# Moving layernorm preparation into the QKV loop, mask setup to GpSimd, and PSUM buffers between pools

## Chip, cores, metric

The kernel runs on one core of one Trainium2 chip. The metric is the device time of one execution in microseconds (us); lower is better. The profiler records one execution, whose span is 1.7 to 2 us shorter than its device time. Runs that the record marks as slow (over 1.5% above the fastest of the same kernel) are left out. The granted clock is the share of the full TensorE clock that the trace records. In the text TensorE is the matmul engine, VectorE, ScalarE and GpSimd the elementwise ones; profile lines call them PE, DVE, ACT and POOL, and PEld is the load of matmul weights.

## The reference

```
x: 2048 x 640;  h = x + A(layernorm(x));  out = h + B(layernorm(h))

A(x): qkv = x @ wqkv                       # 640 x 1920, 32 heads of 20
      phi(t) = where(t > 0, t + 1, exp(t)) + 1e-6
      kv = sum_s phi(k) v^T ;  z = sum_s phi(k)       # per head
      o  = (phi(q) @ kv) / (phi(q) . z + 1e-6) ;  return o @ wo
B(x): token MLP along the 2048 axis: layernorm, w1 (2048 x 1728), gelu, w2
```

## The kernel before

The kernel is written for a framework that orders the instructions of every engine itself at build time: the order of the source is a priority, an instruction with lower priority may be put earlier if it looks ready, and each engine then runs its list strictly in that order. PSUM is the memory that the matmuls here write to; this program uses eight banks of it. PSUM tiles come from pools; a pool with `bufs=1` lets a new tile begin only when the last reader of the old one is done.

Only the first third, up to the "strips" (`pk^T @ [v | 1]` per head block), matters here. x is handled in four chunks of 512 rows. Each chunk is transposed raw, 20 groups of four transposes in all, each group copied out of PSUM by ScalarE. The layernorm is applied to the transposed data: mean and reciprocal deviation are broadcast over the partitions by a matmul with ones, copied out, then subtracted and multiplied in by VectorE.

```
with psT bufs=2, psM bufs=1 (tiles psMb, psRb):            # banks 0-3
    for n in range(4):                                      # chunk
        for c in range(5):
            psT = ...; 4 x nc.tensor.transpose(psT, x_nat ...)
            nc.scalar.activation(out=xnT[n][:, c], in_=psT, Copy)
        RHSM = mean * ident ; RHSR = rstd * ident           # VectorE
        matmul(psMb, ones, RHSM); Mb[n] = copy(psMb)        # ScalarE copy
        matmul(psRb, ones, RHSR); Rb[n] = copy(psRb)
        xnT[n] -= Mb[n] ; xnT[n] *= Rb[n]                   # VectorE
psQ bufs=4 (banks 0-3), psK bufs=1 (4-5), psV bufs=1 (6-7)
def phi_evac(psum, dst):
    tp = max(psum, 0) + 1e-6          # VectorE
    e  = exp(psum)                    # ScalarE
    dst = min(e, 1) + tp              # VectorE
for n in range(4):
    for tt in range(4):               # tile of 128 rows
        psK = 5 + 5 matmuls; phi_evac(psK, pk[t])
        psV = 5 + 5 matmuls; Vpp[t] = copy(psV)             # ScalarE
        js = [tt] if tt < 3 else [tt, 4]                    # five Q groups per chunk
        for j in js: psQ = 5 matmuls; phi_evac(psQ, pqT[n][:, j])
    if n == 1: build_masks()          # memsets on VectorE, selects on GpSimd
# ... cut ...
psStrip (5 one-bank tiles, banks 0-4): for k in 16: for i in 5: matmul(strip[i], pk[k], Vpp[k])
KVd, ZBd = strips * Mask              # VectorE
```

## Time and profile before

| reading | value | view |
|---|---|---|
| time | 295.12 us, median of 6 | runs |
| span of the profiled run | 293.1 us | page |
| TensorE / VectorE / ScalarE busy | 86% / 58% / 35% | page, part 1 |
| first K matmul | 25.67 us | timeline |
| first K result read by VectorE | 34.37 us | timeline |
| first Q matmul | 34.78 us | timeline |
| strips begin | 98.81 us | timeline |

The two groups of the MLP, which the change does not touch, are the largest. They come from part 5 of the page: line, engine, operation, output from inputs, shape, count, then busy us and mean ns, then idle us before it and what ended that idle time.

```profile
L381 PE MATMUL pu<-hn,w_sb 128*128 128x512 bf16 (+1 forms) x448 | 62.9, 304 | 5.3 <-DVE hn L352 5.3
L405 PE MATMUL py<-uT,w_sb 128*128 128x512 bf16 x448 | 64.2, 299 | 0.9 <-ACT xb L384 0.9
```

The front is best read from the timeline: start, duration, engine, source line, operation, count of merged instructions, and in brackets the idle time before it with what ended it. First ScalarE and VectorE up to the first K matmul, then what TensorE does.

```profile
13.40 1.05 ACT L163 ACTIVATE xnT_122<-psT 128x512 bf16<-128x512 bf16 x2
14.65 1.08 ACT L163 ACTIVATE xnT_122<-psT 128x512 bf16<-128x512 bf16 x2 [0.19 <-PE psT L162]
...
19.88 0.30 ACT L140 ACTIVATE rstd_78<-MV_77,eps_t 128x12 f32<-128x12 f32 x1 [4.14 <-DVE msq L135]
21.80 1.49 DVE L174 TENSOR_TENSOR xnT_122<-xnT_122,Mb_126 128x2560 bf16<-128x2560 bf16 x1
23.80 1.49 DVE L176 TENSOR_TENSOR xnT_122<-xnT_122,Rb_130 128x2560 bf16<-128x2560 bf16 x1
25.67 0.81 PE L227 MATMUL psK<-wqkv,xnT_122 128*128 128x512 bf16 x3
...
33.28 0.59 PE L235 MATMUL psV<-wqkv,xnT_122 128*128 128x512 bf16 x2 [1.56 <-ACT Vpp L240]
34.37 0.82 DVE L188 TENSOR_SCALAR tp<-psK 128x640 bf16<-128x640 f32 x1
```

The first chunk's subtraction (L174) runs at 21.80 and its multiplication (L176) at 23.80, and K starts at 25.67. The K result, complete at about 27.8, is read at 34.37, because VectorE works through the later chunks' preparation in between. The end of the QKV part:

```profile
95.02 2.32 PE L246 MATMUL psQ<-xnT_125,wqkv 128*128 128x512 bf16 x10
...
98.81 0.23 PE L271 MATMUL strip_1108<-Vpp,pk 128*128 128x168 bf16 x1 [1.47 <-ACT e L191]
```

The last two Q groups run back to back (10 matmuls in 2.32 us), and the strips then wait 1.47 us, until the last Q has been read.

### The profile page before, as it was taken

To read this page: it belongs to the slowest core of one execution; us is meant where nothing else is said; L and a number is where in the kernel's file an instruction comes from. 1 tells how busy PE (TensorE), PEld (TensorE's weight loads), DVE (VectorE), ACT (ScalarE), POOL (GpSimd) and SP (SyncE) were. 2 spreads that over 40 slices of the span, in tenths; PEclk is the share of its full clock that TensorE was granted. 3 is DMA by queue.
4 is the path that set the end of the run, shared out by engine and by line. 5 is a ranking of instruction groups with operands and counts; after the bars stand their busy time and mean duration, and the time that the engine had idled before them with its cause. 6 is when DMAs were issued, how large, how long until landed. Compare 5 with 4: busy or idle time off the path is not lost.

```text
span 293.1 us, 4250 instructions
## 1 busy us (share of the span) xinstructions
PE 253.1 (86%) x1736; PEld 136.8 (47%) x1736; DVE 171.3 (58%) x326; ACT 102.3 (35%) x166; POOL 26.2 (9%) x42
## 2 busy tenths in 40 slices
PE   0149799999999766998882999999998999999994
PEld 0125454555555642444441555555555555555552
DVE  3799997997787436887887554454544321222221
ACT  2949845545554202751224543334333000000000
POOL 8100070000000100003335000000000000000000
PEclk9999999999999997999997799999999999999998
DMA  6990000000000299100001994000000011110111
GB/s 216 362 229 1 2 1 19 0 0 2 0 0 2 58 425 421 65 0 2 0 0 17 392 410 154 0 0 2 0 2 0 22 47 45 47 45 35 35 45 45
DMA packets 13058, 23.07 MB, mean 79 GB/s; under 512 B 4304, under 2 KB 9136, under 8 KB 13040
## 3 DMA queue, kind: packets, MB, share of 16 engines
q1 hardware_dynamic: 4960, 12.41, 11.8%
q0 software_dynamic: 5216, 6.96, 8.6%
q10 hardware_dynamic: 2864, 3.44, 3.3%
q8 instruction: 13, 0.21, 0.3%
q14 instruction: 5, 0.04, 0.0%
HBM read 20.06 MB, written 2.62 MB: 77 GB/s over the span
## 4 chain that ended last, share of the span: by engine, by line
PE 73%; DVE 12%; ACT 7%; DMA 4%; POOL 2%; issue 2%; ACTq 0%; DVEq 0%
PE py L405 22%; PE pu L381 21%; PE psQ L246 5%; PE psV L235 4%; PE psK L227 4%; PE psN L317 4%; PE pa L329 4%; DMA x_nat<-in_A_x_dram 4%; DVE tp L188 2%; ACT e L191 2%; POOL h_nat L337 2%; PE psR L311 2%; DVE RDENQ L301 1%; PE psK L230 1%; PE psV L238 1%
## 5 line engine op out<-in xcount | busy, mean ns | idle before, releaser
L381 PE MATMUL pu<-hn,w_sb 128*128 128x512 bf16 (+1 forms) x448 | 62.9, 304 | 5.3 <-DVE hn L352 5.3
L405 PE MATMUL py<-uT,w_sb 128*128 128x512 bf16 x448 | 64.2, 299 | 0.9 <-ACT xb L384 0.9
L381 PEld LDWEIGHTS <-w_sb 128*128 128x128 bf16 (+1 forms) x448 | 35.3, 100 | 32.8 <-issue 7.7
L405 PEld LDWEIGHTS <-w_sb 128*128 128x128 bf16 x448 | 33.1, 97 | 32.0 <-issue 9.3
L408 DVE SCALAR_TENSOR_TENSOR ot<-py,b2col,h_nat 128x640 bf16<-128x640 f32 x16 | 14.1, 884 | 48.1 <-PE py L405 48.1
L162 PE MATMUL psT<-ident,x_nat 128*128 128x128 bf16 x80 | 9.4, 263 | 13.6 <-DMA x_nat<-in_A_x_dram 6.8
L384 ACT ACTIVATE xb<-pu,b1col 128x640 bf16<-128x640 f32 (+1 forms) x14 | 11.1, 794 | 20.9 <-PE pu L381 20.9
L162 PEld LDWEIGHTS <-x_nat 128*128 128x128 bf16 x80 | 7.3, 120 | 21.3 <-issue 13.6
L191 ACT ACTIVATE e<-psK 128x640 bf16<-128x640 f32 x16 | 11.3, 703 | 14.4 <-DVE tp L188 14.3
L191 ACT ACTIVATE e<-psQ 128x512 bf16<-128x512 f32 x20 | 12.0, 598 | 11.8 <-DVE tp L188 11.8
L192 DVE SCALAR_TENSOR_TENSOR pk<-e,tp 128x640 bf16<-128x640 bf16 x16 | 13.1, 817 | 5.1 <-ACT e L191 4.9
L337 POOL TENSOR_TENSOR h_nat<-hpre,x_nat 128x640 bf16<-128x640 bf16 x8 | 11.2, 1394 | 45.9 <-ACT hpre L336 45.9
L313 ACT ACTIVATE rexp<-psR 128x512 bf16<-128x512 f32 x20 | 11.7, 596 | 9.9 <-PE psR L311 9.8
L188 DVE TENSOR_SCALAR tp<-psK 128x640 bf16<-128x640 f32 x16 | 13.1, 820 | 2.5 <-PE psK L230 1.9
L188 DVE TENSOR_SCALAR tp<-psQ 128x512 bf16<-128x512 f32 x20 | 13.6, 686 | 0.5 <-PE psQ L246 0.4
L240 ACT ACTIVATE Vpp<-psV 128x640 bf16<-128x640 f32 x16 | 11.2, 703 | 4.9 <-PE psV L238 4.9
L246 PEld LDWEIGHTS <-wqkv 128*128 128x128 bf16 x100 | 9.1, 98 | 8.0
L336 ACT ACTIVATE hpre<-pa 128x640 bf16<-128x640 f32 x8 | 5.6, 703 | 20.3 <-PE pa L329 20.3
L393 DVE TENSOR_SCALAR th<-th 128x640 bf16<-128x640 bf16 (+1 forms) x14 | 4.6, 327 | 11.2 <-ACT th L392 11.2
L317 PEld LDWEIGHTS <-KVd 128*128 128x128 bf16 x52 | 5.3, 103 | 8.8 <-issue 4.0
L395 DVE TENSOR_TENSOR uT<-th,xb 128x640 bf16<-128x640 bf16 (+1 forms) x14 | 6.9, 492 | 0.5
L271 PEld LDWEIGHTS <-pk 128*128 128x128 bf16 x80 | 5.9, 97 | 1.9 <-issue 1.8
(277 smaller groups left out, 373.1 us busy)
## 6 DMA issues: line engine op xcount, KB each, us to landing
w_sb<-in_B_w_dram SPq DMA_DIRECT2D x1, 3584.0 KB, 18.7
w_sb<-in_B_w_dram SPq DMA_DIRECT2D x1, 3456.0 KB, 20.9
w_sb<-in_B_w_dram POOLq DMA_DIRECT2D x1, 3456.0 KB, 19.1
w_sb<-in_B_w_dram POOLq DMA_DIRECT2D x1, 3072.0 KB, 20.6
wqkv<-in_A_wqkv_dram SPq DMA_DIRECT2D x1, 2400.0 KB, 17.8
x_nat<-in_A_x_dram ACTq DMA_DIRECT2D x2, 640.0 KB, 8.8
x_nat<-in_A_x_dram SPq DMA_DIRECT2D x2, 640.0 KB, 7.8
out_dram<-ot SPq DMA_DIRECT2D x8, 160.0 KB, 1.8
```

The lines of the kernel that those rows point to most:

```text
L162: nc.tensor.transpose(psT[:, tt * P:(tt + 1) * P], x_nat[:, t, c * P:(c + 1) * P], ident[:])
L188: nc.vector.tensor_scalar(out=tp[:, 0:cols], in0=psum_ap, scalar1=0.0, scalar2=1e-6, op0=ALU.max, op1=ALU.add)
L191: nc.scalar.activation(out=e[:, 0:cols], in_=psum_ap, func=ACT.Exp)
L192: nc.vector.scalar_tensor_tensor(out=dst_ap, in0=e[:, 0:cols], scalar=1.0, in1=tp[:, 0:cols], op0=ALU.min, op1=ALU.add)
L227: nc.tensor.matmul(psK[:, 0:CH], lhsT=xn[:, c, tsl], rhs=wqkv[:, c, D:D + CH], start=(c == 0), stop=(c == NC - 1))
L235: nc.tensor.matmul(psV[:, 0:CH], lhsT=xn[:, c, tsl], rhs=wqkv[:, c, 2 * D:2 * D + CH], start=(c == 0), stop=(c == NC - 1))
L246: nc.tensor.matmul(psQ[:, :], lhsT=wqkv[:, c, j * P:(j + 1) * P], rhs=xn[:, c, :], start=(c == 0), stop=(c == NC - 1))
L317: nc.tensor.matmul(psN[:, :], lhsT=KVd[:, i, P * j:P * (j + 1)], rhs=pqT[n][:, i, :], start=(a == 0), stop=(a == len(ii) - 1))
L337: nc.gpsimd.tensor_tensor(out=h_nat[:, t, :], in0=hpre[:], in1=x_nat[:, t, :], op=ALU.add)
L381: nc.tensor.matmul(pu[:Mm, c0:c1], lhsT=w1_sb[:, k, m * P:m * P + Mm], rhs=hn[:, k, c0:c1], start=(k == 0), stop=(k == NT - 1))
L405: nc.tensor.matmul(py[:, c0:c1], lhsT=w2_sb[:Kk, k, t * P:(t + 1) * P], rhs=uT[:Kk, k, c0:c1], start=(k == 0), stop=(k == NF - 1))
L408: nc.vector.scalar_tensor_tensor(out=ot[:], in0=py[:, 0:D], scalar=b2col[:, t:t + 1], in1=h_nat[:, t, :], op0=ALU.add, op1=ALU.add)
```

## The change

The intent: let QKV start while later chunks are still being prepared, and take mask setup off VectorE. Chunks 0 and 1 are prepared ahead of the loop, chunks 2 and 3 inside it. The PSUM pools must now live at the same time, and all eight banks are taken: transposes go from two buffers to one, Q accumulators from four to one.

```
+    nc.gpsimd.memset(KVd[:], 0.0)      # ... ZBd, Mask, EselP, selects, DMAs: all on GpSimd, at the start
...
+    psT_pool = ...(name="psT", bufs=1)      # was 2
+    psM_pool = ...(name="psM", bufs=1)      # psMb, psRb: two banks, as before
+    psQ_pool = ...(name="psQ", bufs=1)      # was 4
+    psK_pool, psV_pool = ... bufs=1         # as before
+    for n in range(NCH):                    # all transposes and their copies, before the square roots
+        for c in range(NC): ...
     nc.scalar.activation(out=rstd1a ...Sqrt) ; reciprocal ; rstd1 likewise
+    for m in (0, 1): prep_rhs(m); prep_mm(m); prep_sub(m); prep_mul(m)
     for n in range(NCH):
+        m = n + 2
         for tt in range(TPC):
             ... K, V, Q as before ...
-        if n == 1: build_masks()
+            if m < NCH:
+                if tt == 0:   prep_rhs(m)
+                elif tt == 1: prep_mm(m); prep_sub(m)
+                elif tt == 2: prep_mul(m)
```

More of the change, by code (lines that the diff above doesn't have):

```diff
@@ L83 @@
     EselP = [pC.tile([P, NC, P], BF, name=f"EselP{q}") for q in range(NQ)]
+    nc.gpsimd.memset(KVd[:], 0.0)
+    nc.gpsimd.memset(ZBd[:], 0.0)
+    nc.gpsimd.memset(Mask[:], 1.0)
+    for i in range(NC):
+        mv = Mask[:, i, :].rearrange("p (h e) -> p h e", e=Dh + 1)
+        nc.gpsimd.affine_select(out=mv, in_=mv, pattern=[[-Dh, HPB], [0, Dh + 1]],
+                                compare_op=ALU.is_ge, fill=0.0, base=P * i - Dh * h0[i],
+                                channel_multiplier=1)
+        nc.gpsimd.affine_select(out=mv, in_=mv, pattern=[[Dh, HPB], [0, Dh + 1]],
+                                compare_op=ALU.is_ge, fill=0.0, base=Dh * h0[i] + Dh - 1 - P * i,
+                                channel_multiplier=-1)
+    for q in range(NQ):
+        nc.gpsimd.memset(EselP[q][:], 0.0)
+    nc.gpsimd.memset(EselP[0][0:H], 1.0)
+    for j in range(NC):
+        ev = EselP[0][0:H, j, :]
+        nc.gpsimd.affine_select(out=ev, in_=ev, pattern=[[1, P]], compare_op=ALU.is_ge, fill=0.0,
+                                base=P * j, channel_multiplier=-Dh)
+        nc.gpsimd.affine_select(out=ev, in_=ev, pattern=[[-1, P]], compare_op=ALU.is_ge, fill=0.0,
+                                base=Dh - 1 - P * j, channel_multiplier=Dh)
+    for q in range(1, NQ):
+        nc.gpsimd.dma_start(out=EselP[q][q * H:(q + 1) * H, :, :], in_=EselP[0][0:H, :, :])
     esR1 = ctx.enter_context(ExitStack())
@@ L137 @@
                                    in1=msq[:], op0=ALU.mult, op1=ALU.subtract)
-    nc.scalar.activation(out=rstd1a[:, :], in_=MVa[:, 1, :], func=ACT.Sqrt, bias=eps_t[:], scale=1.0)
-    nc.vector.reciprocal(out=rstd1a[:, :], in_=rstd1a[:, :])
-    nc.scalar.activation(out=rstd1[:, 0:NDV], in_=MV1[:, 0:NDV, 1:2], func=ACT.Sqrt, bias=eps_t[:], scale=1.0)
-    nc.vector.reciprocal(out=rstd1[:, 0:NDV], in_=rstd1[:, 0:NDV])
     def mean_ap(n):
@@ L151, in rstd_ap @@
         return rstd1a[:, :, None]
-    with tc.tile_pool(name="psT", bufs=2, space=bass.MemoryType.PSUM) as psT_pool, \
-            tc.tile_pool(name="psM", bufs=1, space=bass.MemoryType.PSUM) as psM_pool:
-        for n in range(NCH):
-            xn = xnT[n]
-            tsl_n = slice(n * TPC, (n + 1) * TPC)
-            for c in range(NC):
-                psT = psT_pool.tile([P, CH], BF, name="psT")
-                for tt in range(TPC):
-                    t = n * TPC + tt
-                    nc.tensor.transpose(psT[:, tt * P:(tt + 1) * P], x_nat[:, t, c * P:(c + 1) * P], ident[:])
-                nc.scalar.activation(out=xn[:, c, :], in_=psT[:, :], func=ACT.Copy)
-            nc.vector.tensor_tensor(out=RHSM[:, tsl_n, :], in0=mean_ap(n).to_broadcast([P, TPC, P]),
-                                    in1=ident[:, None, :].to_broadcast([P, TPC, P]), op=ALU.mult)
-            nc.vector.tensor_tensor(out=RHSR[:, tsl_n, :], in0=rstd_ap(n).to_broadcast([P, TPC, P]),
-                                    in1=ident[:, None, :].to_broadcast([P, TPC, P]), op=ALU.mult)
-            psMb = psM_pool.tile([P, CH], F32, name="psMb")
-            nc.tensor.matmul(psMb[:, :], lhsT=ones_bf[:, :], rhs=RHSM[:, tsl_n, :], start=True, stop=True)
-            nc.scalar.activation(out=Mb[n][:, :], in_=psMb[:, :], func=ACT.Copy)
-            psRb = psM_pool.tile([P, CH], F32, name="psRb")
-            nc.tensor.matmul(psRb[:, :], lhsT=ones_bf[:, :], rhs=RHSR[:, tsl_n, :], start=True, stop=True)
-            nc.scalar.activation(out=Rb[n][:, :], in_=psRb[:, :], func=ACT.Copy)
-            nc.vector.tensor_tensor(out=xn[:], in0=xn[:], in1=Mb[n][:, None, :].to_broadcast([P, NC, CH]),
-                                    op=ALU.subtract)
-            nc.vector.tensor_tensor(out=xn[:], in0=xn[:], in1=Rb[n][:, None, :].to_broadcast([P, NC, CH]),
-                                    op=ALU.mult)
-            if "xnT" in dbg:
-                nc.sync.dma_start(out=dbg["xnT"].rearrange("(c p) s -> p c s", p=P)[:, :, n * CH:(n + 1) * CH],
-                                  in_=xn[:])
@@ L182 @@
-    psQ_pool = esR4.enter_context(tc.tile_pool(name="psQ", bufs=4, space=bass.MemoryType.PSUM))
+    psT_pool = esR4.enter_context(tc.tile_pool(name="psT", bufs=1, space=bass.MemoryType.PSUM))
+    psM_pool = esR4.enter_context(tc.tile_pool(name="psM", bufs=1, space=bass.MemoryType.PSUM))
+    psQ_pool = esR4.enter_context(tc.tile_pool(name="psQ", bufs=1, space=bass.MemoryType.PSUM))
     psK_pool = esR4.enter_context(tc.tile_pool(name="psK", bufs=1, space=bass.MemoryType.PSUM))
     psV_pool = esR4.enter_context(tc.tile_pool(name="psV", bufs=1, space=bass.MemoryType.PSUM))
+    for n in range(NCH):
+        for c in range(NC):
+            psT = psT_pool.tile([P, CH], BF, name="psT")
+            for tt in range(TPC):
+                t = n * TPC + tt
+                nc.tensor.transpose(psT[:, tt * P:(tt + 1) * P], x_nat[:, t, c * P:(c + 1) * P], ident[:])
+            nc.scalar.activation(out=xnT[n][:, c, :], in_=psT[:, :], func=ACT.Copy)
@@ new lines, with prep_rhs @@
+    nc.scalar.activation(out=rstd1a[:, :], in_=MVa[:, 1, :], func=ACT.Sqrt, bias=eps_t[:], scale=1.0)
+    nc.vector.reciprocal(out=rstd1a[:, :], in_=rstd1a[:, :])
+    nc.scalar.activation(out=rstd1[:, 0:NDV], in_=MV1[:, 0:NDV, 1:2], func=ACT.Sqrt, bias=eps_t[:], scale=1.0)
+    nc.vector.reciprocal(out=rstd1[:, 0:NDV], in_=rstd1[:, 0:NDV])
+    def prep_rhs(m):
+        tsl_n = slice(m * TPC, (m + 1) * TPC)
+        nc.vector.tensor_tensor(out=RHSM[:, tsl_n, :], in0=mean_ap(m).to_broadcast([P, TPC, P]),
+                                in1=ident[:, None, :].to_broadcast([P, TPC, P]), op=ALU.mult)
+        nc.vector.tensor_tensor(out=RHSR[:, tsl_n, :], in0=rstd_ap(m).to_broadcast([P, TPC, P]),
+                                in1=ident[:, None, :].to_broadcast([P, TPC, P]), op=ALU.mult)
@@ new lines, in prep_mm @@
+    def prep_mm(m):
+        tsl_n = slice(m * TPC, (m + 1) * TPC)
+        psMb = psM_pool.tile([P, CH], F32, name="psMb")
+        nc.tensor.matmul(psMb[:, :], lhsT=ones_bf[:, :], rhs=RHSM[:, tsl_n, :], start=True, stop=True)
+        nc.scalar.activation(out=Mb[m][:, :], in_=psMb[:, :], func=ACT.Copy)
+        psRb = psM_pool.tile([P, CH], F32, name="psRb")
+        nc.tensor.matmul(psRb[:, :], lhsT=ones_bf[:, :], rhs=RHSR[:, tsl_n, :], start=True, stop=True)
+        nc.scalar.activation(out=Rb[m][:, :], in_=psRb[:, :], func=ACT.Copy)
@@ new lines, in prep_sub, with prep_mul @@
+    def prep_sub(m):
+        xn = xnT[m]
+        nc.vector.tensor_tensor(out=xn[:], in0=xn[:], in1=Mb[m][:, None, :].to_broadcast([P, NC, CH]),
+                                op=ALU.subtract)
+    def prep_mul(m):
+        xn = xnT[m]
+        nc.vector.tensor_tensor(out=xn[:], in0=xn[:], in1=Rb[m][:, None, :].to_broadcast([P, NC, CH]),
+                                op=ALU.mult)
+        if "xnT" in dbg:
+            nc.sync.dma_start(out=dbg["xnT"].rearrange("(c p) s -> p c s", p=P)[:, :, m * CH:(m + 1) * CH],
+                              in_=xn[:])
@@ L193, in phi_evac @@
                                        op0=ALU.min, op1=ALU.add)
-    def build_masks():
-        nc.vector.memset(Mask[:], 1.0)
-        for i in range(NC):
-            mv = Mask[:, i, :].rearrange("p (h e) -> p h e", e=Dh + 1)
-            nc.gpsimd.affine_select(out=mv, in_=mv, pattern=[[-Dh, HPB], [0, Dh + 1]],
-                                    compare_op=ALU.is_ge, fill=0.0, base=P * i - Dh * h0[i],
-                                    channel_multiplier=1)
-            nc.gpsimd.affine_select(out=mv, in_=mv, pattern=[[Dh, HPB], [0, Dh + 1]],
-                                    compare_op=ALU.is_ge, fill=0.0, base=Dh * h0[i] + Dh - 1 - P * i,
-                                    channel_multiplier=-1)
-        for q in range(NQ):
-            nc.vector.memset(EselP[q][:], 0.0)
-        nc.vector.memset(EselP[0][0:H], 1.0)
-        for j in range(NC):
-            ev = EselP[0][0:H, j, :]
-            nc.gpsimd.affine_select(out=ev, in_=ev, pattern=[[1, P]], compare_op=ALU.is_ge, fill=0.0,
-                                    base=P * j, channel_multiplier=-Dh)
-            nc.gpsimd.affine_select(out=ev, in_=ev, pattern=[[-1, P]], compare_op=ALU.is_ge, fill=0.0,
-                                    base=Dh - 1 - P * j, channel_multiplier=Dh)
-        for q in range(1, NQ):
-            nc.sync.dma_start(out=EselP[q][q * H:(q + 1) * H, :, :], in_=EselP[0][0:H, :, :])
-        nc.vector.memset(KVd[:], 0.0)
-        nc.vector.memset(ZBd[:], 0.0)
+    for m in (0, 1):
+        prep_rhs(m)
+        prep_mm(m)
+        prep_sub(m)
+        prep_mul(m)
     for n in range(NCH):
@@ L248 @@
                 phi_evac(psQ[:, :], pqT[n][:, j, :], CH)
-        if n == 1:
-            build_masks()
+            if m < NCH:
+                if tt == 0:
+                    prep_rhs(m)
+                elif tt == 1:
+                    prep_mm(m)
+                    prep_sub(m)
+                elif tt == 2:
+                    prep_mul(m)
         if "pqT" in dbg:
```

## The prediction

> **What bounds the kernel now.** From the page: TensorE is busy 86% of a 293.1 us span, VectorE 58%, ScalarE 35%. The chain of waits gives 43% to the two MLP matmul groups (62.9 and 64.3 us), which the change leaves alone. Only the front, up to about 106 us, can move. Its timeline:
> - 0 to 25.5 us: loads of x (last landing 12.2 us), then VectorE's row statistics, which end at 19.8; square root, reciprocal, broadcast, subtract and multiply let the first QKV matmul start at 25.5.
> - 25.5 to 34.8 us: VectorE is busy 9.31 of 9.32 us, largely with subtract and multiply (1.49 us each) of later chunks. The first K result, finished at 27.8, is not read until 34.4. TensorE is busy 7.64 us, with one hole of 1.56 us. No Q matmul runs before 34.8: the Q accumulators reuse the banks of the transposes and broadcasts, and start just after the last broadcast is copied out.
> - 34.8 to 98.2 us: TensorE busy 62.3 of 63.4 us. Then 1.47 us of waiting before the KV strips.
>
> Recoverable TensorE idle is about 1.7 + 1.1 + 1.5 = 4.3 us.
>
> **What the change does.** It removes VectorE memsets inside QKV (0.59 + 1.39 + 0.12 us) and puts masks on the idle GpSimd. They are needed only at about 104 us, so this is nearly worthless. The Trainium skill (Perfetto Trace Analysis, Optimizing Scalar/DVE Operations) warns that GpSimd and VectorE share an SBUF port; here statistics took 0.44 to 0.48 us with and without GpSimd selects beside them, so I expect no harm.
>
> It moves the subtract/multiply of chunks 2 and 3 (about 4.3 us each with their small products) into the QKV loop, and lets Q start at once. I credit 2 us: the hole and the late start.
>
> It pays in PSUM: Q accumulators go from 4 to 1, transposes from 2 to 1. The skill (same page, Matmuls) says independent groups should rotate through banks so that eviction overlaps the next group. A Q round trip: 1.08 matmul + 0.69 VectorE + 0.60 ScalarE (after VectorE, on the same tile) + about 0.5 of hand-overs = 2.9 us; five Qs per four tiles make 3.6 us per tile, against TensorE's 4.1 (estimates). It fits on average, without slack for a 1.49 us subtract in between. I charge 2 us of stalls over the loop, 1 us for transposes waiting on single-buffer copies, and 1.5 us at the tail, where the last two Qs run back to back and the second must wait for the first's eviction.
>
> Statistics, the start at 25.5 and everything after the strips stay.
>
> **Sum.** 295.1 - 2 - 0.5 (memsets) + 2 + 1 + 1.5, rounded down because QKV order can fill holes: 296. Range 290.5 to 302. Faster by over 2%: 0.05; within 2%: 0.80; slower by over 2%: 0.15.
>
> **What would show it.** First K matmul still at 25 to 26.5 us; first K result read by 28.5; Q matmuls before 30; subtracts of chunks 2 and 3 between 30 and 65. The waits list should show Q matmuls waiting on the ScalarE exponential and transposes on their copies, several us together. Strips begin at 98 to 101 us. MLP groups unchanged at 63 and 64 us. GpSimd masks done by 25 us.
>
> **What would make it wrong.** If the freed banks let strip matmuls be placed inside QKV, or Q eviction hides completely, the gain is 3 to 5 us. If the instruction order is built for faster evictions than the chip gives, TensorE waits in order at each Q: 20 times 0.5 us would be 10 us. If square roots queue behind all the transposes' copies, the start slips by several us.

## The result

The changed kernel took 302.21 us (median of 20 runs, 300.11 to 304.59) against 295.19 us (40 runs): ratio 1.0239, 95% interval 1.0218 to 1.0259. Ratios here are the mean time of one kernel's fast runs over that of the other's of the same rounds, so not quite the ratio of the medians. A later measurement on another occasion (the last experiment) gave 300.74 us and 1.0194; the difference is taken up below. The profiled run has a span of 299.1 us, 6.0 over before.

The MLP groups in part 5 of the page of the changed kernel are as they were:

```profile
L399 PE MATMUL pu<-hn,w_sb 128*128 128x512 bf16 (+1 forms) x448 | 63.3, 305 | 5.2 <-DVE hn L370 5.2
L423 PE MATMUL py<-uT,w_sb 128*128 128x512 bf16 x448 | 64.3, 299 | 0.9 <-ACT xb L402 0.9
```

The timeline of the changed kernel, the same places as before:

```profile
13.59 0.58 ACT L181 ACTIVATE xnT_153<-psT 128x512 bf16<-128x512 bf16 x1
...
20.07 0.30 ACT L184 ACTIVATE rstd_78<-MV_77,eps_t 128x12 f32<-128x12 f32 x1 [5.90 <-DVE msq L157]
20.28 0.58 ACT L181 ACTIVATE xnT_153<-psT 128x512 bf16<-128x512 bf16 x1
...
24.08 0.60 ACT L181 ACTIVATE xnT_153<-psT 128x512 bf16<-128x512 bf16 x1 [0.20 <-PE psT L180]
24.71 1.49 DVE L205 TENSOR_TENSOR xnT_153<-xnT_153,Mb_157 128x2560 bf16<-128x2560 bf16 x1 [0.22 <-ACT xnT_153 L181]
26.24 1.49 DVE L210 TENSOR_TENSOR xnT_153<-xnT_153,Rb_161 128x2560 bf16<-128x2560 bf16 x1
28.15 0.81 PE L239 MATMUL psK<-wqkv,xnT_153 128*128 128x512 bf16 x3
...
31.46 0.82 DVE L218 TENSOR_SCALAR tp<-psK 128x640 bf16<-128x640 f32 x1
```

Only one copy (L181) is through before the square root (L184), where before there were four. The other groups of chunk 0 follow one at a time after 20 us, so the first subtraction (L205) comes at 24.71 instead of 21.80, and the first K matmul at 28.15, 2.48 us late. The first K result is now read at 31.46, 2.9 us earlier than before. The interleaving was meant to do that, but this alone does not show that it did: e2 below, with no interleaving, reads it at 31.63. The clean pair is e7 and e6, 34.57 and 28.07. The end, again from the timeline:

```profile
99.16 1.24 PE L258 MATMUL psQ<-xnT_156,wqkv 128*128 128x512 bf16 x5
101.88 1.24 PE L258 MATMUL psQ<-xnT_156,wqkv 128*128 128x512 bf16 x5 [1.47 <-ACT e L221]
104.59 0.23 PE L289 MATMUL strip_1108<-Vpp,pk 128*128 128x168 bf16 x1 [1.47 <-ACT e L221]
```

The last two Q groups are torn apart by 1.47 us, the time in which the single accumulator is read by VectorE and then by ScalarE. The strips begin at 104.59 instead of 98.81: 5.78 of the 6.0 us of span are lost before the strips.

Where in the stretch from first K to first strip? The busy time by windows gives it; each line is a window, its length, then the busy us (and count) of PE, PEld, DVE, ACT and POOL, then TensorE's granted clock, DMA share and GB/s. Before:

```profile
25.67:34.78 9.11, 7.43 (x63) 4.29 (x62) 9.10 (x9) 8.11 (x17) 0.00 (x0) 1.00 0.01 3
34.78:98.81 64.03, 62.29 (x395) 32.24 (x394) 52.92 (x76) 32.81 (x52) 5.29 (x10) 1.00 0.01 3
```

The changed kernel:

```profile
28.15:48.76 20.61, 19.98 (x152) 11.11 (x150) 17.90 (x20) 15.46 (x26) 0.00 (x0) 1.00 0.00 1
48.76:104.59 55.83, 50.77 (x318) 25.96 (x317) 41.02 (x59) 25.74 (x41) 0.00 (x0) 1.00 0.00 1
```

Before: 73.14 us with TensorE busy 69.72, so 3.42 idle. Changed: 76.44 us, busy 70.76 (19.98 + 50.77, rounded), idle 5.68. So 5.78 us = 2.48 (late start) + 2.26 (more idle) + 1.04 (more busy). The last term is not work that moved: by windows for their source lines alone, transposes after the first K matmul are busy 4.38 us against 3.06 before, but the broadcast matmuls 0 against 1.30, which cancels it. The rest is in the QKV matmuls themselves (V 28.59 us against 27.93, K 27.76 against 27.26, Q 24.99 against 24.51; these overlap each other a little). They are the same matmuls in more and shorter pieces, and a piece is counted longer alone: two Q groups are busy 2.32 us in one run and 1.24 each when torn apart. So part of the cost of the stalls is counted as busy, and "idle" understates it.

### The profile page after: what moved, and what is told of

The parts are those of the page before. It is cut to its first block, busy times and chain, and to the rows that moved or that the text cites. A ratio compares the mean times of both kernels' runs of the same rounds, so it can differ in the third digit from the quotient of the medians.

```text
span 299.1 us, 4239 instructions
## 1 busy us (share of the span) xinstructions
PE 254.3 (85%) x1736; PEld 136.2 (46%) x1736; DVE 168.2 (56%) x318; ACT 103.3 (35%) x166; POOL 31.5 (11%) x53
## 4 chain that ended last, share of the span: by engine, by line
PE 70%; DVE 13%; ACT 8%; DMA 4%; issue 2%; POOL 2%; ACTq 0%; DVEq 0%
PE py L423 21%; PE pu L399 21%; PE psQ L258 5%; PE psN L335 4%; PE psK L239 4%; PE pa L347 4%; ACT e L221 4%; DMA x_nat<-in_A_x_dram 4%; DVE tp L218 4%; PE psV L247 3%; POOL h_nat L355 2%; PE psT L180 2%; PE psR L329 1%; DVE RDENQ L319 1%; DVE h_nat L350 1%
## 5 line engine op out<-in xcount | busy, mean ns | idle before, releaser
L399 PE MATMUL pu<-hn,w_sb 128*128 128x512 bf16 (+1 forms) x448 | 63.3, 305 | 5.2 <-DVE hn L370 5.2
L423 PE MATMUL py<-uT,w_sb 128*128 128x512 bf16 x448 | 64.3, 299 | 0.9 <-ACT xb L402 0.9
L180 PE MATMUL psT<-ident,x_nat 128*128 128x128 bf16 x80 | 8.7, 238 | 15.1 <-ACT xnT_153 L181 7.5
L180 PEld LDWEIGHTS <-x_nat 128*128 128x128 bf16 x80 | 6.6, 105 | 27.2 <-issue 18.8
L282 POOL DMA_DIRECT2D w_sb<-in_B_w_dram x1 | 0.9, 941 | 86.6 <-DVE pqT_141 L222 86.6
L258 PE MATMUL psQ<-xnT_156,wqkv 128*128 128x512 bf16 x25 | 6.2, 378 | 1.8 <-ACT e L221 1.8
```

What stands on the lines that cost most here:

```text
L180: nc.tensor.transpose(psT[:, tt * P:(tt + 1) * P], x_nat[:, t, c * P:(c + 1) * P], ident[:])
L258: nc.tensor.matmul(psQ[:, :], lhsT=wqkv[:, c, j * P:(j + 1) * P], rhs=xn[:, c, :], start=(c == 0), stop=(c == NC - 1))
L399: nc.tensor.matmul(pu[:Mm, c0:c1], lhsT=w1_sb[:, k, m * P:m * P + Mm], rhs=hn[:, k, c0:c1], start=(k == 0), stop=(k == NT - 1))
L423: nc.tensor.matmul(py[:, c0:c1], lhsT=w2_sb[:Kk, k, t * P:(t + 1) * P], rhs=uT[:Kk, k, c0:c1], start=(k == 0), stop=(k == NF - 1))
```

## The experiments

Two theories. **Buffers**: the loss is the price in PSUM; one transpose buffer delays the start, one Q accumulator stalls the loop and tears the tail. **Interleaving**: the moved subtractions block evictions on VectorE, or the GpSimd work slows it, or the moved square roots delay the start. TensorE's recorded dips all lie behind the strips (last section), so the time at which the strips begin is free of them and is used beside the total. It comes from one profile per kernel; the changed kernel, profiled twice, repeated it to 0.03 us (104.59 and 104.62, e12). One clock effect remains in it. The clock entries stored in a trace begin with a rise to full clock, and until then matmuls are slower: 128x512 broadcasts that stand alone take 0.58 to 0.63 us before the rise and 0.38 after it, in both kernels, although the windows view, which has no entry there, prints 1.00. The rise comes at 24.65 us in the kernel before and at 24.61 in the changed one, so it does not touch their comparison; in the others it comes between 23.6 (e9) and 26.9 us (e6), but at 31.3 us in e4. Differences of a few tenths of a us between experiments can come from it. "Stretch" is first K to first strip, "idle" the stretch less TensorE's busy time, by windows as above.

| run | edit | ratio to before | first K | strips | stretch | idle |
|---|---|---|---|---|---|---|
| before | | 1 | 25.67 | 98.81 | 73.14 | 3.42 |
| changed | | 1.0239, 1.0194 | 28.15 | 104.59 | 76.44 | 5.68 |
| e1 | before, one Q buffer | 1.0246 | 25.92 | 104.71 | 78.79 | 8.28 |
| e2 | before, masks moved | 0.9982 | 26.45 | 98.66 | 72.21 | 3.26 |
| e3 | changed, two transpose buffers | 1.0132 | 26.62 | 102.59 | 75.97 | 6.13 |
| e4 | changed, two Q buffers | 1.0087 | 29.26 | 101.74 | 72.48 | 2.76 |
| e5 | changed, fifth Q moved | 1.0139 | 28.28 | 103.47 | 75.19 | 4.13 |
| e6 | interleaved, shared pool | 0.9914 | 26.20 | 97.40 | 71.20 | 1.81 |
| e7 | before, shared pool | 0.9950 | 26.33 | 98.04 | 71.71 | 2.02 |
| e8 | e6 and fifth Q moved | 0.9987 | 26.16 | 98.00 | 71.84 | 2.37 |
| e9 | before, one transpose buffer | 1.0155 | 27.17 | 102.77 | | |
| e11 | e6 and split strips | 0.9827 | 26.01 | 95.35 | | |

(e10 is the first run of the kernel of e11, e12 a repeat of the changed kernel.) All results were correct.

### e1: the kernel before with one Q accumulator

```
-    psQ_pool = tile_pool(name="psQ", bufs=4)
+    psQ_pool = tile_pool(name="psQ", bufs=1)
-    psQ = psQ_pool.tile([P, CH], F32)
+    psQ = psQ_pool.tile([P, 4 * CH], F32)[:, 0:CH]     # keeps the same four banks
```

> Kernel before, with one Q accumulator in place of four (it still occupies the same four banks, so nothing else moves). Theory (the single Q accumulator costs): the last two Qs are torn apart by a hole of about 1.5 us, some stalls before; strips begin 2.5 to 4.5 us later than 98.8, total 2.5 to 4.5 us over before. Rival (Q eviction hides, the loss lies in the front only): within 0.7 us of before.

302.44 us against 295.36, ratio 1.0246 (1.0206 to 1.0287). The strips begin at 104.71, 5.90 us late, more than was expected, although K starts where it did before. This edit alone, with none of the interleaving, costs as much as the whole change. Waits of TensorE between 25 and 105 us (engine, line, what it waited for: us in total, times, longest), in the kernel before:

```profile
PE psV L235 <- ACT Vpp L240: 1.6, 1, 1.6
PE strip_1108 L271 <- ACT e L191: 1.5, 1, 1.5
...
```

in e1:

```profile
PE psQ L246 <- ACT e L191: 2.5, 4, 1.5
PE psV L235 <- ACT Vpp L240: 2.4, 2, 1.6
PE strip L271 <- ACT e L191: 1.5, 1, 1.5
PE psK L227 <- ACT e L191: 0.8, 2, 0.6
```

and in the changed kernel:

```profile
PE psQ L258 <- ACT e L221: 2.2, 3, 1.5
PE strip_1108 L289 <- ACT e L221: 1.5, 1, 1.5
PE psV L247 <- ACT Vpp L252: 0.8, 1, 0.8
PE psK L239 <- ACT e L221: 0.7, 2, 0.5
...
```

The Q waits for ScalarE's exponential, absent before, are there in both; the longest, 1.5 us, is the hole between the last two Q groups. V and K wait more as well in e1; a likely reason, not tested by itself, is that with no free Q accumulator the order of TensorE's list has less to fill with. TensorE is idle 8.28 us in e1's stretch against 3.42. Of these 4.86 us, 2.5 are Q waits (1.5 of them the hole at the tail), 1.4 more waits of V and K, and the rest gaps too short for the list.

The round trip behind it can be read off the end of the timeline: the last Q but one ends at about 100.5 us, VectorE reads it from 100.57 on, ScalarE from 101.36, and the last Q starts at 102.00. The two reads never overlap. The Trainium skill (PSUM — Partial Sum Buffer, Terms) says that two engines must not touch one bank in the same 32 partitions at the same time, reads included. The trace agrees: for all 20 Q and 16 K results of e1, ScalarE's read begins at least 0.09 us after VectorE's has ended.

### e2: the kernel before with only the masks moved

```
+    nc.gpsimd.memset(KVd[:], 0.0)   # ... the changed kernel's mask block, at the same early place
-        if n == 1: build_masks()
```

> Kernel before, with only the mask setup moved to GpSimd and to the start. Theory (masks are off the critical path): within 0.7 us of before; statistics still end near 19.8 us. Rival (GpSimd work beside VectorE's statistics slows them or delays the start): start of QKV and total 1 us or more later.

294.93 us, ratio 0.9982 (0.9953 to 1.0011). The strips begin 0.15 us earlier. Statistics end at 19.88 (19.85 before). The rebuilt order starts K 0.8 us later and loses that much less in the loop. Masks are neither a gain nor a cost in total. But ScalarE has only two copies through before the square root here, not four, although nothing but the masks moved; this matters for e9 below.

### e3 and e4: giving the changed kernel one buffer back

One bank is won by letting the two broadcast tiles share a bank, and spent on transposes (e3) or on Q (e4).

```
-    psMb = psM_pool.tile([P, CH], F32, name="psMb") ; psRb = ... name="psRb"
+    psMb = psM_pool.tile([P, CH], F32, name="psMR") ; psRb = ... name="psMR"
e3:  psT bufs=1 -> 2          e4:  psQ bufs=1 -> 2
```

> Changed kernel, with two transpose buffers again (the two broadcast tiles share one bank to pay for it). Theory (the single transpose buffer delays the start): first K matmul returns from 28.2 to 25.5 to 26.5 us and the total falls by 1.5 to 3 us against the changed kernel (ratio to before about 1.015). Rival (the start is late because of the moved square roots or the masks): first K stays near 28 us, total unchanged within 0.7 us.

> Changed kernel, with two Q accumulators (the two broadcast tiles share one bank to pay for it). Theory: the hole of 1.5 us between the last two Qs goes and the Q waits in the loop too; total falls by 2.5 to 3.5 us against the changed kernel (ratio to before about 1.013), first K still near 28 us. Rival (the loop is slow because the moved subtracts block VectorE): hole at the end goes (1.5 us), the rest of the loop stays.

e3: 299.46 us, ratio 1.0132. First K at 26.62, just outside the expected range: 1.53 of the 2.48 us come back (with the broadcasts now sharing a bank), and the strips begin 2.0 us earlier. e4: 297.96 us, ratio 1.0087. The hole in the tail is gone, no Q wait is left among the listed waits, idle falls from 5.68 to 2.76 us, and the stretch from 76.44 to 72.48. The total fell by more than was expected (ratio about 1.013). K starts even later, at 29.26, and not near 28: the broadcasts now share a bank, transposes still have one buffer, and TensorE reaches full clock only at 31.3 us here (24.6 in the changed kernel), so that a round of transpose and copy takes 1.27 us up to then, against 1.07 after the rise in the changed kernel. So, with the shared broadcast bank included, the second Q accumulator is worth about 4.0 us of stretch in the changed kernel, rather more than less because the slow clock reaches 2 us into the stretch, and the rival of e4 (only the hole of 1.5 us would go) falls.

### e5: the fifth Q group of each chunk moved

```
-    js = [tt] if tt < TPC - 1 else [tt, TPC]
+    js = [tt, TPC] if tt == 0 else [tt]
```

> Changed kernel, with the extra (fifth) Q group of each chunk put after the chunk's first tile instead of after its last; banks untouched. Theory (single Q accumulator, one hole of 1.47 us between the last two Qs): the hole at the end goes, first K stays at 28.2 us; total falls by 1 to 2 us against the changed kernel if the waits inside the loop stay. Rival (the last chunk is bound by something else): strips begin at 104.6 us as before the edit.

300.15 us, ratio 1.0139. The hole at the end is gone and the strips begin 1.12 us earlier; the listed Q waits in the stretch are 1.6 us, in six pieces of at most 0.4. A change of order buys back part of what the buffer cost. The mean of the total, 299.9 us, is 1.1 us under that of the changed kernel's repeat (301.0) and 2.3 us under that of its first measurement (302.2), with the clock on its side: four of five runs here had a granted clock of 0.989.

### e6, e7, e8: one shared pool, with and without interleaving

Transposes, broadcasts and Q all take one bank, so they can rotate through one pool of four.

```
-    psT_pool (1), psM_pool (2), psQ_pool (1)
+    psQ_pool = tile_pool(name="psQ", bufs=4)      # psT, psMb, psRb, psQ all from it, one tag
e6:  interleaved; square roots first; each chunk's transposes emitted with its own preparation
e7:  the kernel before, pools merged in the same way, nothing interleaved
e8:  e6 with js = [tt, TPC] if tt == 0 else [tt]
```

> Changed kernel's interleaving with the PSUM price taken out: transposes, broadcasts and Q rotate through one pool of four one-bank buffers, roots stand where they stood before, and each chunk's transposes are emitted with its own preparation. Theory (the interleaving itself is worth about 2 us and only the buffers cost): first K at 25 to 26 us, first K result read within 1.5 us of its end, strips at 95.5 to 97.5 us, total 1 to 3 us below the kernel before (ratio 0.990 to 0.997). Rival (interleaving itself costs, as subtracts block evictions): at or above the kernel before.

> Kernel before with only the pools merged (transposes, broadcasts and Q share four one-bank buffers), nothing interleaved. It tells the interleaving apart from the shared pool. Theory (the hole before 34.8 us comes from VectorE being full of chunk preparation): within 1 us of the kernel before. Rival (the hole came from the Q pool waiting for the broadcast pool): 1 to 2 us faster than before, as much as the interleaved version with the same pool.

> As the interleaved version with the shared pool, with the extra Q group moved to the chunk's first tile. With four buffers the last two Qs already run back to back, so the theory expects no gain: within 0.7 us of the version without the move. Rival (the order of Q matters by itself): 1 us or more faster.

e6: 293.13 us, ratio 0.9914 (0.9892 to 0.9936), faster than before by 2.5 us. First K comes at 26.20, 0.2 us outside the expectation, its result is read at 28.07, and the strips begin at 97.40, as expected. Its waits of TensorE between 20 and 105 us show no wait of a Q matmul on ScalarE. The busy time by windows in e6:

```profile
26.20:48.00 21.80, 21.80 (x152) 11.95 (x153) 19.93 (x25) 13.92 (x24) 0.00 (x0) 1.00 0.01 2
48.00:97.40 49.40, 47.59 (x315) 25.09 (x314) 39.62 (x55) 27.65 (x46) 0.00 (x0) 1.00 0.00 1
```

Up to 48 us TensorE has no idle time left. e7: 294.12 us, ratio 0.9950 (0.9928 to 0.9971), 1.5 us faster than before (0.9 to 2.1 by the interval): probably outside the 1 us that my theory allowed and, by strips, 0.77 us earlier. So of e6's gain more than half is the shared pool, and the interleaving adds 0.64 us at the strips (98.04 to 97.40) and 0.9 us of mean time (294.17 to 293.23). The first is a little too small: e6 reached full clock 0.5 us later than e7, at 26.85 us, and its first five K matmuls took 1.56 us (1.25 in e11, which starts like e6). My belief that interleaving alone was worth about 2 us does not hold in this form. e8: 295.36 us, slower than e6 by 2.2 us, where I expected no difference. Only 0.6 us of it lie before the strips (a wait of 2.08 us in place of 1.47); the rest goes with a lower recorded clock (last section).

### e9: the kernel before with one transpose buffer

```
-    psT bufs=2 ; psT = tile([P, CH], BF)
+    psT bufs=1 ; psT = tile([P, 4 * CH], BF), first CH used      # keeps the same two banks
```

> Kernel before, with one transpose buffer in place of two (it still occupies the same two banks). Theory (the single transpose buffer alone makes the start late): first K matmul at 27.5 to 29 us instead of 25.7. The total will rise by more than this start, since the Q pool of this kernel opens only when the transposes are done (expected at about 40 us): 2 to 5 us over before. Rival (the late start of the changed kernel came from its moved roots and reordering): first K within 0.7 us of 25.7.

300.44 us, ratio 1.0155. First K at 27.17, 1.5 us later than before, and then the next K matmul only at 28.45: less than expected, more than the rival allowed. The Q pool of this kernel opens when the transposes are done, at 41.56 us here, so the total holds that delay too and says nothing of the changed kernel. Together with e3 (1.53 us back) the single buffer accounts for about 1.5 of the 2.48 us. The moved square roots account for nothing: with them put back where they stood, the built program of the changed kernel has the same instructions in the same order on all five engines, so that kernel was not run. Most of the remaining 1 us goes with the masks, by way of the built order: moving them alone starts K at 26.45 with two copies ahead of the square root (e2), and the changed kernel with two transpose buffers, at 26.62 with two copies ahead (e3), starts almost like it. (In both TensorE reaches full clock at 25.5 us, 0.9 later than before, which may be part of it.) That leaves about 0.2 us for the new order of emission (all chunks' transposes first), which was not varied by itself.

### e10, e11: a cure for the wait before the strips

Every run above shows 1.47 us or more of waiting before the strips.

```
 (from e6)
-    pools in the order Q, K, V ; one pool of five strips ; for k: for i: matmul(strip[i])
+    pools in the order V, K, Q ; four strips in the banks of V and K, the fifth in a bank of Q
+    for i: for k: matmul(strip[i])
```

> The interleaved version with the shared pool, plus a cure for the hole of 1.47 us before the strips, which every run so far shows: V and K accumulators take the first four banks, four of the five strips follow in those banks, the fifth in a Q bank, and strips are built one after the other. Expected: strips begin within 0.3 us of the last Q matmul (at about 96 us), the first psDen matmul comes 1.5 to 2.5 us earlier than in the version it starts from, total 1 to 2.5 us below that version (ratio to before 0.983 to 0.988). If the pools wait as a whole, nothing moves.

> The same kernel as in the run before (split strips), once more, because that run's one profiled execution was an outlier (544 us, TensorE instructions at about half speed at a recorded clock of 1.0) while its five timed ones lay between 289.4 and 291.6 us. Expected: a profile of about 288.5 us, strips beginning within 0.3 us of the last Q matmul at about 96 us, ratio to before 0.980 to 0.985. If the outlier belongs to the kernel, it comes again.

e10: the five timed runs lie between 289.41 and 291.62 us, ratio 0.9824 (0.9793 to 0.9855), but its profiled execution took 544.35 us; it is not used for any comparison of kernels. e11 gave 289.80 us (288.97 to 290.77), ratio 0.9827 (0.9805 to 0.9849), and a clean profile; the outlier did not come again. The timeline of e11 around the strips:

```profile
93.19 2.32 PE L258 MATMUL psQ<-xnT,wqkv 128*128 128x512 bf16 x10
95.35 5.98 PE L291 MATMUL strip<-Vpp,pk 128*128 128x168 bf16 x80
101.27 2.35 PE L316 MATMUL psDen<-pqT,ZBd 128*32 128x512 bf16 x20
```

No idle time is noted before the strips (L291), nor before the next group, psDen (L316), which begins at 101.27 against 104.95 in e6. The masking of each finished strip now runs under the next strip, so the gain of 3.7 us at psDen is larger than the hole; 0.4 us of it come from further in front (the last two Qs begin at 93.19, against 93.60 in e6). This version beats both kernels: 5.5 us under before, 11 us under the change.

### e12: the changed kernel again

> The changed kernel as it is, on this chip, beside the best version. Expected: ratio 1.020 to 1.026; strips at 104.6 us again. The timed runs of the first measurement fell into groups by granted clock (about 300.5 us at 0.98, 302.8 us at 0.975): if that grouping is real, it shows again, with runs at 0.98 about 5 us over the runs of before at the same clock.

300.74 us, ratio 1.0194 (1.0172 to 1.0216), first K at 28.20 and strips at 104.62, as in the first profile. In the first measurement 13 of the 21 listed executions had a granted clock of 0.975 or less and averaged 303.1 us; the eight at 0.98 or 0.981 averaged 300.6. Here only one of six was at 0.975, with 302.07 us, the others averaging 300.7. So the grouping shows again, if by a single run, and the ratio depends on how many runs fall into the lower group: the ratio here is just under my expectation and under 2%. Runs at 0.979 to 0.981 are 5.2 us over those of the kernel before at that clock (300.75 against 295.59), as expected. What comes from the schedule is the 5.8 us before the strips; the rest of the first 7.0 us goes with the clock.

## Why the prediction was wrong

The predicted 296 us was 6 us low. Two steps failed. The larger is the price of the single Q accumulator: "2 us of stalls over the loop" and 1.5 us at the tail were charged, and paid alone it delays the strips by 5.9 us (e1). The other is "the start at 25.5 ... stays": the first K moved 2.48 us, because three of the four copies that ScalarE had made before the square root now came after it. Point by point:

- **What bounds the kernel, and that only the front moves: right.** MLP groups 63.3 and 64.3 us (62.9 and 64.2 before); 5.78 of 6.0 us lost before the strips.
- **Masks nearly worthless, no harm: right for the total** (e2, ratio 0.9982), but not for the start, which they delay by 0.8 us through the built order. The 0.5 us credited to them is neither shown nor refuted: e2 ended 0.4 us lower, within the noise, with strips 0.15 us earlier.
- **"The start at 25.5 ... stays": wrong.** It moved to 28.15. I had charged 1 us for single-buffered transposes, but as waits in the loop, not on the path to the first K. The step that failed is looking at ScalarE's list: only one copy was placed ahead of the square root that waits for the statistics, and four groups of chunk 0 were left for after 20 us, about 1.3 us apart. One buffer alone (e9) and the masks alone (e2) each leave two of the four copies ahead; together they leave one. The buffer explains about 1.5 us (e3, e9), the masks' place about 0.8 (e2). The risk I did name, the square roots behind all copies, was the wrong one: their place changes nothing in the built order.
- **Credit of 2 us for the hole and the late Q: the size holds inside this change.** With Q single-buffered in both, the stretch is 78.79 us without (e1) and 76.44 with the other edits (changed), 2.35 us less. With four shared buffers in both, interleaving is worth only 0.5 us of stretch (e7 to e6), because the shared pool already takes the hole.
- **Q's price, 2 us in the loop and 1.5 at the tail: right in kind, wrong where most of it falls.** The tail hole is 1.47 us as charged. In the loop TensorE's listed waits for Q itself are only 1.0 us in e1; more went to V and K (1.4 us more than before), to short gaps (about 1 us) and to more busy time (0.8 us), none of which I charged. The whole price is 5.9 us in the old kernel (e1) and about 4.0 in the changed one (e4). The average I leaned on (3.6 us of Q round trip against 4.1 of TensorE per tile) says nothing of a fixed order: K, V and Q now each had a single accumulator, and a late read of one can stall whatever stands next in TensorE's list. That reading fits the waits of V and K; no run isolates it.
- **"Rounded down because QKV order can fill holes": wrong, and no measurement behind it.** The terms added to 297.1; I took off 1.1.
- **Listed waits: right in kind.** Q on the exponential 2.2 us; transposes on copies 0.6 us after 25 us, together not "several". Strips expected at 98 to 101, were at 104.59; first K result by 28.5, read at 31.46; Q before 30, first at 32.48. Subtractions of chunks 2 and 3 lie between 30 and 65 as foreseen (37.34 and 42.82), masks were done by 25.
- **The clock was left out.** About 1.2 us: 7.0 in the first measurement less the 5.8 before the strips.

One path from the old kernel to the changed one adds up, by the strips' start: Q alone +5.90 us (e1), then the other edits +2.23 (first K from 25.92 to 28.15) and -2.35 (stretch from 78.79 to 76.44), together +5.78. Against my sum that is Q 2.4 us over the 3.5 charged, the start 1.2 over the 1 charged, the credits right to 0.2, the rounding 1.1, the clock 1.2: together 6.1 of the 6.2 us missed. That it closes so well is in part luck: the credits agree as a sum only, and the masks' share of them is not shown. The order of the path matters (Q is worth 4.0 when it is given back last, in e4), and what share of the idle time in the loop belongs to the moved subtractions, and not to Q, was not separated.

## What to carry to other kernels

When a change needs PSUM banks, price what gives them up by doing that alone in the old kernel: one Q accumulator instead of four cost as much as the whole change here. The Trainium skill's advice to rotate independent groups through different banks (Perfetto Trace Analysis, Optimizing Tensor Performance, Matmuls) held here with numbers, and a shared pool of one-bank tiles kept the rotation for phases that hardly overlap. In an engine's fixed list, a single buffer upstream can put its copies behind an unrelated wait, so read the order of the eviction engine's list, not the average load; and a wait at a phase boundary can be taken away by placing the next phase's tiles in banks that are freed first.

## What the Trainium skill lacked or had wrong

- TensorE: Matmul & The Clock Gate, Part 1, says the clock falls to half after at least one idle window of about 3.4 us. Here a dip came with shorter gaps: before the first dip of the kernel before (113.4 to 116.8 us) the longest TensorE wait nearby was 2.15 us, ended at 112.45, and in the 3.41 us just before the dip TensorE was busy 0.90. A later section of the page (A second HAM failure mode: psum-queue depth-cycling) does say that frequent short idles between groups make the clock swing, but it names no gap or busy share at which they do. The length agrees: dips of 3.4 us (e6, 112.2 to 115.6) and 6.8 us (e8, 111.3 to 118.1) are one and two windows. Part 2 of the profile page shows the clock in tenths for 40 slices; e6, then e8:

```profile
PEclk9999999999999997999999799999999999999998
```

```profile
PEclk9999999999999995999998699999999999999999
```

- The same page calls the window free-running and the effect variable from run to run. That fits the groups of the changed kernel (clock 0.98 and exactly 0.975, 2.2 us apart). It does not explain why all six executions of e8 stood at 0.974 or 0.975 and all six of e6 at 0.98 to 0.988, though the two kernels differ by 0.6 us at the strips; this stays open.
- I found no page that describes the outlier of e10 (544.35 us): TensorE at less than half speed for the whole execution, other engines unchanged. Its recorded clock of 1.0 means only that the trace holds no clock entry at all; all other traces hold a rise to full clock at 23.6 to 31.3 us. So it looks like a rise that never came, which one run can't show. The same page warns of unreliable clock records and of a gate stuck low for over 50 us, and gives half speed as 427 ns between 512-wide matmuls; here five of a Q group took 2.33 us from start to start of the next, so 466 ns (1.08 us for five, 216 ns, in the other runs at full clock). Mean durations of the same group (part 5 form), e10 and then e11:

```profile
L401 PE MATMUL pu<-hn,w_sb 128*128 128x512 bf16 x200 | 117.3, 673 | 5.2 <-DVE hn L372 5.2
```

```profile
L401 PE MATMUL pu<-hn,w_sb 128*128 128x512 bf16 x200 | 56.7, 386 | 5.2 <-DVE hn L372 5.2
```

- Perfetto Trace Analysis, Optimizing Scalar/DVE Operations, warns of the SBUF port that GpSimd and VectorE share. No run here shows a loss: in the changed kernel statistics took 0.44 to 0.48 us each beside a busy GpSimd, and e2 ended at 0.9982.
